# Key turns of the second head group ahead of the scaling of the value results on VectorE

## The chip, the cores and the metric

The kernel runs on one core of one Trainium2 chip. The metric is the device time of a run in microseconds (us), from the first to the last instruction with what the launch adds; the time of a kernel is the median of several runs.

## The reference

Two layers are applied twice to a small state `x` of 4 sequences with one token each (D = 512): attention against a cache of keys and values, then a gated feed-forward. The second round uses the same weights and the same caches.

```python
def _A_ref(x, k_cache, v_cache, wq, wo):          # 32 query heads, 8 key/value heads
    q = (x @ wq).reshape(B, Sq, Hq, Dh) ...        # Dh = 128
    scores = jnp.einsum("bhqd,bhkd->bhqk", q, k) * (Dh ** -0.5)   # 4096 cached keys
    p = _softmax(scores, axis=-1)
    o = jnp.einsum("bhqk,bhkd->bhqd", p, v)
    return o.reshape(B, Sq, Hq * Dh) @ wo
def _B_ref(x, w_gate, w_up, w_down):               # F = 1792
    return (_gelu(x @ w_gate) * (x @ w_up)) @ w_down

x = x + _A_ref(_layernorm(x), ...)
x = x + _B_ref(_layernorm(x), ...)
x = x + _A_ref(_layernorm(x), ...)
x = x + _B_ref(_layernorm(x), ...)
```

## The kernel before

All data is bfloat16. The caches of one sequence hold 8 heads of 4096 x 128 elements each for keys and for values, 8 MB apiece, and are the bulk of what is moved: 114 MB in all. The kernel works sequence by sequence and interleaves the second attention of one sequence with the first attention of the next, so that the keys and values stream without a long stop. `attend(b2, b1, ...)` (line 523) does this for the pair: `b2` is the sequence in its second attention (none in the first call), `b1` the next one in its first. It is called four times, for `b1` = 0 to 3; these calls are "attention 0" to "attention 3" here. The eight key/value heads go in two groups of four; `ga` and `gb` are the first and second group of `b1`. `attend_last` and `dense` do the last second attention and the feed-forward.

Keys and values are cut into tiles of 512 KB: half of one head of one sequence, `t` = 0 or 1. A key tile comes from DMA with the keys along the partitions, and VectorE turns it in place, as 32-bit words in blocks of 32 x 32: `Keys.turn` (line 373, the instruction on line 378, one for each tile, in the order in which tiles were loaded). For the second group this order is head by head, both halves of a head together, so the eight turns are (head 0, t 0), (head 0, t 1), (head 1, t 0) and so on. `scores(sc, g, t)` (line 383) then multiplies the four heads' halves t by the queries: 16 matmuls on line 389. The four of each round go over the four heads, so the first half, t = 0, needs the turns number 1, 3, 5 and 7, and the second half needs number 8 as well.

`soft` (line 393) takes the maximum on VectorE and the exponential on ScalarE, `soft_turn` and `soft_swap` bring the probabilities into the layout of the values, and `Values.step(n)` (line 492) makes n value units: one unit is one value tile times its probabilities, 16 matmuls on line 506 into the accumulator `ot`, of which there are two. After every fourth unit (after every second near the end of a sequence) VectorE scales the accumulated result by the reciprocal of the softmax sum and writes it to `OT_bf`: line 514. `out_proj` (line 276) reads `OT_bf` later.

Value tiles are loaded into a ring of seven tiles (`load_v`, line 467). A load is issued on the single DMA queue as soon as a slot is free, and a slot is freed when the unit that read it is done (`release`, line 464). Key tiles have places of their own and are loaded again when the scores that read them are done.

The order of instructions on each engine is the order in which the code names them; nothing rearranges it (`tc.manual_schedule()`, line 81). [...]

The place of the change is the middle of `attend`, lines 599 to 604. Ahead of it, turns 1 and 2 of the second group have been made, the softmax of the first group is done, and the queries for the second group are built. Line 599 makes turn 3, line 600 makes five value units on TensorE with one scaling on VectorE behind the fourth, line 601 makes turns 4 to 7, line 603 the first half of the scores, line 604 turn 8.

Of the kernel before, what the change touches and what calls it, by code (L numbers as in the profile page):

```python
# [30 lines left out]
def kernel(  # L31
# [224 lines left out]
    def build_q1(b, g):  # L256
        q_build(q_spread(q1_bf[:, g, :, b], amask, g), g)
# [95 lines left out]
    class Keys:  # L353
# [19 lines left out]
        def turn(self, count=1):  # L373
            for _ in range(count):
                kvh, t = self.tile(self.nt)
                self.nt += 1
                words = KT[kvh][t].rearrange("p c d -> p (c d)").bitcast(FP32)
                nc.vector.transpose(out=words, in_=words)  # L378

    def new_scores(bank):  # L380
        return ps_sc.tile([P, CH, QS], FP32, name="sc", tag=f"sc{bank}")
# [141 lines left out]
    def attend(b2, b1, next_q=None, rest=None):  # L523
# [4 lines left out]
        turn = keys.turn  # L528
# [67 lines left out]
        if first:  # L596
            q_first(q_rows(0, B, 1), 1, rstd1)
        build_q1(b1, gb)
        turn()
        vals.step(5)  # L600
        turn(4)
        sc1 = new_scores(0)
        scores(sc1, gb, 0)
        turn()
# [99 lines left out]
    x_bf = tmpp.tile([P, D], BF16, name="x_bf", tag="pp")  # L704
    dq.dma_start(out=x_bf[:B, :], in_=A_x.flatten_outer_dims())
    proj, prev = attend(None, 0)
    for b in range(B):
        fill = (lambda n: None) if prev is None else prev.step
        dense(b, 1, proj, fill)
        ln_square(b, 1)  # L710
        fill(1)
        mv = ln_center(b, 1)
        fill(1)
        ga, gb = groups(b + 1)
        qr0 = q_rows(b, 1, ga)
        rstd = ln_rstd(1, mv)
        am = small.tile([P, QD], FP32, name="am", tag="am")
        nc.vector.tensor_scalar(out=am[:], in0=amask[:], scalar1=rstd[:, 0:1], scalar2=None,
                                op0=ALU.mult)
        qm0 = q_spread(turn_rows(qr0, 512)[:, :, 0], am, ga)  # L720
        fill(2)
        q_build(qm0, ga)
        fill(1)

        def next_q():
            return q_spread(turn_rows(q_rows(b, 1, gb), 512)[:, :, 0], am, gb)

        if b < B - 1:
            proj, prev = attend(b, b + 1, next_q, fill)
        else:  # L730
            proj = attend_last(b, next_q, fill)
# [41 lines left out]
```

## Time and profile before

Three runs took 338.26, 335.23 and 338.08 us; the median is 338.08 us. The profiled execution has a span of 337.1 us, to which all profile times refer.

| what | us | number | mean ns |
|---|---|---|---|
| key turns, VectorE, L378 | 75.4 | 64 | 1218 |
| value units, TensorE, L506 | 62.8 | 1920 matmuls | 166 |
| scores, TensorE, L389 | 62.0 | 512 matmuls | 535 |
| scalings of value results, VectorE, L514 | 6.5 | 40 | 163 |
| VectorE idle ahead of L514 | 41.9 | | |
| VectorE idle ahead of L378 | 3.4 | | |
| TensorE idle ahead of L389 | 25.1 | | |
| DMA, share of 16 engines | 86.9% | 113.53 MB | |

"Busy" sums the durations of instructions; matmuls overlap in the array, so 16 of them take less than 16 times their mean. "Idle ahead of" an instruction is the time in which its engine did nothing just before it, put down to what ended it. In the timelines, a row merges instructions of one line that follow each other; its columns are start, duration, engine, line, operation, tiles, count, and in brackets the idle time ahead with its releaser. In the chain of waits the columns are start, duration and what ran. The memory traffic comes to 337 GB/s over the span, and to some 410 to 420 GB/s where nothing stops it.

### The profile page before, as it was taken

The page shows a single profiled execution, that of the slowest core. Times are in us where ns is not written, and L with a number is a line of the kernel's source. Part 1 is how long each engine was busy: PE and PEld are TensorE (multiplying, and loading weights), DVE is VectorE, ACT ScalarE, POOL GpSimd, SP SyncE. Part 2 cuts the span into 40 slices and gives each one's busy share as a digit, 9 for nine tenths or more (in the row PEclk, how much of TensorE's full clock was granted, in tenths as well). Part 3 has the DMA queues.
Part 4 walks back from the last instruction along what each step waited for, and adds up shares of the span by engine and source line. Part 5 has one row for each costly group of instructions (what it writes and reads, how often), then busy time and mean ns, then how long its engine had stood idle before and what let it go on. Part 6 is the DMA issues. An engine that isn't in the chain of part 4 may idle for free.

```text
span 337.1 us, 8603 instructions
## 1 busy us (share of the span) xinstructions
PE 209.5 (62%) x3844; PEld 121.4 (36%) x3844; DVE 171.1 (51%) x481; ACT 29.1 (9%) x70; POOL 0.7 (0%) x6
## 2 busy tenths in 40 slices
PE   1343275243587144989874539799763378798875
PEld 0011234121334122466441324564511236464655
DVE  5666262013439276425477774354787453544233
ACT  0003001000010010210010103000101012001100
POOL 0000000000000000000000000000000000000000
PEclk9996555555576555555585555555955575559555
DMA  7999976999759999589989994899999967999920
GB/s 273 423 416 419 412 302 239 351 379 379 304 136 420 419 421 386 218 321 380 366 296 414 421 382 170 318 403 399 370 424 418 416 213 269 410 373 379 413 82 2
DMA packets 27317, 114.07 MB, mean 338 GB/s; under 512 B 2312, under 2 KB 8208, under 8 KB 19984
## 3 DMA queue, kind: packets, MB, share of 16 engines
q1 hardware_dynamic: 27280, 113.53, 86.9%
q8 instruction: 30, 0.49, 0.6%
q14 instruction: 7, 0.06, 0.0%
HBM read 113.51 MB, written 0.00 MB: 337 GB/s over the span
## 4 chain that ended last, share of the span: by engine, by line
DMA 46%; PE 25%; DVE 16%; SPq 8%; issue 2%; ACT 2%; DVEq 0%
DMA ring<-in_A_v_cache_dram 30%; DMA kt<-in_A_k_cache_dram 13%; PE sc L389 8%; PE ot L506 6%; DVE kt L378 5%; DMA wd_sb<-in_B_w_down_dram 3%; SPq L134 3%; SPq L128 3%; PE rows L315 2%; PE y L348 2%; PE rows L226 2%; DVE pp L416 2%; ACT pp L408 1%; PE x L435 1%; DVE rows L216 1%
## 5 line engine op out<-in xcount | busy, mean ns | idle before, releaser
L506 PE MATMUL ot<-pe,ring 128*128 128x4 bf16 x1920 | 62.8, 166 | 35.5 <-DMA ring<-in_A_v_cache_dram 34.6
L506 PEld LDWEIGHTS <-ring 128*128 128x128 bf16 x1920 | 59.9, 105 | 65.1 <-DMA ring<-in_A_v_cache_dram 42.1
L389 PE MATMUL sc<-kt,qb 128*32 128x512 bf16 x512 | 62.0, 535 | 25.1 <-DVE kt L378 22.0
L378 DVE STREAM_TRANSPOSE kt<-kt 128x1024 f32<-128x1024 f32 x64 | 75.4, 1218 | 3.4 <-DMA kt<-in_A_k_cache_dram 3.4
L389 PEld LDWEIGHTS <-qb 128*32 128x32 bf16 x512 | 17.2, 114 | 53.6 <-issue 30.4
L216 DVE STREAM_TRANSPOSE rows<-rows 128x512 f32<-128x512 f32 (+1 forms) x23 | 16.2, 706 | 39.0 <-PE rows L226 19.1
L514 DVE TENSOR_TENSOR OT_bf<-ot,rden 128x8 bf16<-128x8 f32 (+1 forms) x40 | 6.5, 163 | 41.9 <-PE ot L506 41.4
L408 ACT ACTIVATE pp<-sc,nm 128x512 bf16<-128x512 f32 x16 | 11.0, 687 | 181.7 <-DVE junk L404 112.2
L395 DVE TENSOR_REDUCE m<-sc 128x1 f32<-128x512 f32 x16 | 10.8, 678 | 26.5 <-PE sc L389 26.5
L435 PE MATMUL x<-pp,ident_bf 128*32 128x128 bf16 x256 | 9.0, 282 | 22.1 <-DVE pp L416 21.8
L281 PE MATMUL rows<-wo_sb,OT_bf 128*1 128x512 bf16 (+1 forms) x136 | 16.5, 582 | 8.5 <-DMA wo_sb<-in_A_wo_dram 7.3
L226 PE MATMUL rows<-wq_sb,xn_bf 128*1 128x512 bf16 (+1 forms) x160 | 18.0, 595 | 4.6 <-DMA wq_sb<-in_A_wq_dram 4.3
L435 PEld LDWEIGHTS <-ident_bf 128*32 128x32 bf16 x256 | 6.5, 118 | 27.9 <-issue 25.9
L416 DVE STREAM_TRANSPOSE pp<-pp 128x512 bf16<-128x512 bf16 x16 | 11.2, 703 | 7.3 <-ACT pp L408 7.3
L438 ACT CAST pe<-x 128x512 bf16<-128x512 f32 x16 | 9.4, 586 | 18.6 <-PE x L435 18.6
L348 PE MATMUL y<-H_bf,wd_sb 128*128 128x1 bf16 (+1 forms) x280 | 8.6, 166 | 2.8 <-DVE H_bf L341 1.5
L348 PEld LDWEIGHTS <-wd_sb 128*128 128x128 bf16 x280 | 8.1, 104 | 4.1 <-DMA wd_sb<-in_B_w_down_dram 3.1
L247 PE MATMUL qe<-qm,t_bf 128*128 128x64 bf16 x16 | 3.4, 213 | 9.3 <-DVE qm L237 7.1
L250 DVE TENSOR_TENSOR qb<-qe,amask 128x256 bf16<-128x256 f32 x16 | 6.8, 425 | 4.7 <-PE qe L247 4.7
L226 PEld LDWEIGHTS <-xn_bf 128*1 128x1 bf16 (+1 forms) x160 | 4.5, 110 | 12.9 <-issue 11.7
L421 PE MATMUL den<-zx,mean_f 128*128 128x16 f32 x32 | 8.9, 357 | 0.0
L315 PE MATMUL rows<-wu_sb,xn_bf 128*1 128x448 bf16 x64 | 6.7, 567 | 2.9 <-DMA wu_sb<-in_B_w_up_dram 2.9
(78 smaller groups left out, 121.9 us busy)
## 6 DMA issues: line engine op xcount, KB each, us to landing
ring<-in_A_v_cache_dram SPq DMA_DIRECT2D x37, 1024.0 KB, 8.9
ring<-in_A_v_cache_dram SPq DMA_DIRECT2D x44, 512.0 KB, 7.0
kt<-in_A_k_cache_dram SPq DMA_DIRECT2D x20, 1024.0 KB, 14.3
kt<-in_A_k_cache_dram SPq DMA_DIRECT2D x24, 512.0 KB, 8.4
wq_sb<-in_A_wq_dram SPq DMA_DIRECT2D x2, 2048.0 KB, 20.2
wo_sb<-in_A_wo_dram SPq DMA_DIRECT2D x4, 1024.0 KB, 12.2
kt<-in_A_v_cache_dram SPq DMA_DIRECT2D x8, 512.0 KB, 9.8
wg_sb<-in_B_w_gate_dram SPq DMA_DIRECT2D x1, 1792.0 KB
```

What stands on the lines that cost most here:

```text
L216: nc.vector.transpose(out=rows[:, :n], in_=rows[:, :n])
L226: nc.tensor.matmul(rows[j * QS:j * QS + nb, :], lhsT=xn_bf[:, k, bs], rhs=w, start=(k == 0), stop=(k == KD - 1))
L281: nc.tensor.matmul(rows[r0:r0 + lhsT.shape[-1], :], lhsT=lhsT, rhs=wo_sb[:, i, :], start=(start and n < QD), stop=(stop and n >= hp - QD))
L315: nc.tensor.matmul(rows[j * QS:j * QS + nb, :KF * QS], lhsT=xn_bf[:, k, bs], rhs=w[:, j], start=(k == 0), stop=(k == KD - 1))
L348: nc.tensor.matmul(y[:, k], lhsT=wd_sb[:, c, k * P:(k + 1) * P], rhs=H_bf[:, c, :], start=(c == 0 and k == 0), stop=(c == KF - 1), skip_gr ...
L378: nc.vector.transpose(out=words, in_=words)
L389: nc.tensor.matmul(sc[s * QS:(s + 1) * QS], lhsT=qb[:, w0:w0 + 2 * W], rhs=kt[:, :, be // 2, :, be % 2], start=(t == 0 and be == 0), stop= ...
L395: nc.vector.tensor_reduce(out=m[:], in_=sc.rearrange("p c j -> p (c j)"), axis=AX.X, op=ALU.max)
L408: nc.scalar.activation(out=pp[:], in_=sc[:], func=ACT.Exp, bias=nm[:, 0:1], scale=scale, accum_out=ls[:])
L416: nc.vector.transpose(out=flat, in_=flat)
L435: nc.tensor.matmul(x[a * QS:(a + 1) * QS, s], lhsT=ident_bf[:, s * QS:(s + 1) * QS], rhs=pT[:, a], start=True, stop=True, skip_group_check ...
L506: nc.tensor.matmul(self.ot[:, s % 2], lhsT=v[:, i, :], rhs=pe[:, s, c, :], start=(c == 0), stop=(c == C - 1), skip_group_check=True)
```

## The change

The four turns that stood behind the five value units are made ahead of them, together with the one that was there already. TensorE's order stays as it was: five value units, then the first half of the scores. On VectorE the first scaling of value results of each attention comes after turn 7 instead of after turn 3. The aim is that VectorE does not wait for TensorE's value units while it has loaded key tiles to turn.

```diff
         build_q1(b1, gb)
-        turn()
+        turn(5)
         vals.step(5)
-        turn(4)
         sc1 = new_scores(0)
         scores(sc1, gb, 0)
         turn()
```

## The prediction

> **What bounds the kernel now.** I read the page first (engine shares and slices), then the chain of waits, then the timelines of TensorE and VectorE around the four places that the edit touches, and last the DMA rate in those windows. The page says that no engine is full and that the DMA engines come nearest:
>
> ```profile
> PE 209.5 (62%) x3844; PEld 121.4 (36%) x3844; DVE 171.1 (51%) x481; ACT 29.1 (9%) x70; POOL 0.7 (0%) x6
> ...
> q1 hardware_dynamic: 27280, 113.53, 86.9%
> ...
> DMA 46%; PE 25%; DVE 16%; SPq 8%; issue 2%; ACT 2%; DVEq 0%
> ```
>
> DMA is busy for 86.9% of 337.1 us, some 293 us, so about 44 us are left in which it stands still, and the chain that ended last leaves DMA for more than half of its length. The kernel alternates: DMA streams until the value ring is full, then a stretch of TensorE and VectorE work decides when ring slots come free again. A saving counts only in such a stretch. The chain, in order of time, shows one in attention of sequence 1:
>
> ```profile
> 111.16 17.43 DMA ring<-in_A_v_cache_dram
> 128.63 1.03 PE ot L506 x32
> 129.85 4.54 DVE kt L378 x4
> 134.43 1.87 PE sc L389 x13
> 136.30 0.52 PE ot L506 x16
> 136.82 1.85 PE sc L389 x16
> ...
> 143.05 1.44 PE ot L506 x48
> 144.50 7.82 DMA ring<-in_A_v_cache_dram
> ```
>
> Value tiles arrive, TensorE makes the fourth value unit, VectorE then scales (L514) and only then makes four key turns of 1.14 us, and the scores wait for them. The same "DVE kt L378 x4, 4.54" stands in the chain at 41.22, 129.85, 196.55 and 265.82 us: once in each of the four attentions, and nowhere else with that length. The VectorE timeline tells why the turns are late:
>
> ```profile
> 125.30 1.24 DVE L378 STREAM_TRANSPOSE kt<-kt 128x1024 f32<-128x1024 f32 x1
> 129.68 0.17 DVE L514 TENSOR_TENSOR OT_bf<-ot,rden 128x8 bf16<-128x8 f32 x1 [3.15 <-PE ot L506]
> 129.77 5.74 DVE L378 STREAM_TRANSPOSE kt<-kt 128x1024 f32<-128x1024 f32 x5
> ```
>
> VectorE idles 3.15 us for TensorE with the turns standing behind the scaling; the five turns then run without a gap, so their keys had landed. On TensorE it reads:
>
> ```profile
> 131.09 0.59 PE L506 MATMUL ot<-pe,ring 128*128 128x4 bf16 x16 [1.45 <-DMA ring<-in_A_v_cache_dram]
> 131.62 1.15 PE L389 MATMUL sc<-kt,qb 128*32 128x512 bf16 x3
> 134.43 1.87 PE L389 MATMUL sc<-kt,qb 128*32 128x512 bf16 x13 [1.67 <-DVE kt L378]
> 136.23 0.59 PE L506 MATMUL ot<-pe,ring 128*128 128x4 bf16 x16
> 136.75 1.90 PE L389 MATMUL sc<-kt,qb 128*32 128x512 bf16 x16
> ```
>
> [...] loaded keys were not turned in the 3.15 us of waiting. [...] The trace shows 0.50 at all four places until 272 us, so I price matmuls as found there[...].
>
> **The change part by part.** Nothing is added or taken away: VectorE has the same instructions, and in each of four attentions the first scaling of value results moves behind four key turns. TensorE's and the DMA queue's order stay.
>
> (1) The turns. They can start when the turn before the scaling ends. VectorE's idle time before L514 is 6.19, 3.15, 2.06 and 4.97 us at the four places, so that moment is 41.05-6.19 = 34.86, 129.68-3.15 = 126.53, 194.32 and 260.68 us. Four turns take 4.6 us (5.74/5 x 4, with their gaps), so they end at 39.5, 131.1, 198.9 and 265.3 instead of 45.8, 134.4, 201.1 and 270.4. Keys: in attentions 1 to 3 they are queued ahead of value tiles that TensorE had used by those moments; in attention 0 they come just ahead of a value pair used at 37.51, which may hold the turns some us, inside 6.19 us of slack.
>
> (2) The scaling. It now starts at the later of its matmuls and the turns: at 131.1 instead of 129.7 in attention 1, at 198.9 instead of 196.4 in attention 2, unchanged in the others. Who waits for it: its result goes to the output projection, first at 139.52 us in attention 1, some 8 us later, and it frees one of two accumulators, wanted again at the ninth unit, at 143.05. The one turn queued behind it (the eighth tile) ends about 132.4, and the second score half, which needs it, starts after 134. So the delay costs nothing.
>
> (3) The scores. TensorE's fifth value unit still waits for its value tile from DMA, so the first score half still starts at 43.04, 131.62, 198.76 and 267.61. Its 16 matmuls end at 47.67, 136.30, 203.00 and 272.27 by the chain, that is 4.63, 4.68, 4.24 and 4.66 us later. With all keys turned the same 16 take 1.90 us: the second half, at 136.75, shows it. In attention 2 the fourth of them needs a turn that ends 0.1 us after the first starts, which the three ahead of it cover. The saving is 2.73 + 2.78 + 2.34 + 2.76 = 10.6 us, and this is the disputed size: the wait that the trace names is only 1.67 us. I take the difference of the ends, since three early matmuls drawn out over 1.15 us are not 1.15 us of array work when 13 take 1.87.
>
> (4) What follows. Unit 6, the second half, two units, the softmax of L395 to L438 and then the ninth unit all hang in one chain, from 136.3 to 144.5 in attention 1, where the ring's next load is released. Does DMA let this move forward? Two windows of attention 1 tell (start and end, length, busy us and instructions of the five engines, TensorE's clock, DMA share, GB/s):
>
> ```profile
> 126.00:136.00 10.00, 5.27 (x96) 3.05 (x96) 6.36 (x7) 0.00 (x0) 0.00 (x0) 0.50 1.01 396
> 136.00:146.00 10.00, 9.40 (x181) 5.79 (x181) 4.41 (x15) 3.34 (x8) 0.00 (x0) 0.50 0.48 159
> ```
>
> DMA is full up to about 136 and then idle for half of ten us: (1-0.48) x 10 = 5.2 us. The same view of attentions 0, 2 and 3 (48 to 57, 203 to 212 and 272 to 281 us, shares 0.43, 0.41 and 0.46) gives 5.1, 5.3 and 4.9 us. Each is above the 2.3 to 2.8 us to be taken out, so the idle time shrinks to about 2.4 us and the loads after it start earlier by the whole saving. The values used in between are there: the stream up to 136 brings a pair in about 2.46 us (128.63, then 131.09), so units 7 and 8 land near 133.6 and are wanted near 135.9. After each stretch the chain runs on through loads which it released itself, so the four savings add.
>
> Sum: 338.08 - 10.6 = 327.5 us.
>
> **The rivals.** (B) The saving is only the wait that is named. For it: it is the trace's own figure, 1.67 at each place; if the three early matmuls really need their 1.15 us, the rest follows with its 1.87. Against it: the undisturbed 16 in 1.90. Time: 338.08 - 4 x 1.67 = 331.4 us. (C) DMA takes it back: the value stream, full ahead of the stretch, is the true limit, and TensorE only waits for values 2.7 us sooner. For it: 86.9% DMA, 42.1 us of weight loads waiting for the ring. Against it: about 5 us of idle DMA just behind each place. Time: 338.1 us. (D) Keys are late, and the scaling and all behind it wait for them. For it: turns wait for keys 5 times, 3.4 us in total, longest 1.5. Against it: none of these stands at the four places, where turns run on without a gap. If all 3.4 us were added: 341.5 us, slower. (E) [...] In attention 3, where it is granted from 274 on, the way from the first half's end to the next load takes 280.24-272.27 = 7.97 us against 8.20 in attention 1; three more of these give 0.7 us, 326.8 us.
>
> **How the numbers follow.** My forecast with (E), which is inside its width, 0.83; (B) 0.11; (C) 0.03; (D) 0.03. The time is 327.5 us. The range takes in (B) at the top, 331.4, and at the bottom the spread of the three times before: the fastest, 335.23, less 10.6 is 324.6. Low 324.6, high 331.5. Faster by over 1% follows from the forecast, (E) and (B), 0.94; within 1% from (C), 0.03; slower from (D), 0.03.
>
> **What would show it.** In the profile after: VectorE's timeline has four turns, then the scaling, with its idle time nearly gone in attentions 1 and 2; the first score half is 16 matmuls in 1.9 us behind the fifth unit with no wait for L378; the chain has no "DVE kt L378 x4" of 4.54 us there; the idle DMA behind each place is near 2.4 us. Wrong would be a value wait on unit 6 or 7 instead (C), a first half of 3 us (B), or turns waiting for keys (D).

## The result, and the profile after

The changed kernel took 326.22 us (median of four runs, 323.41 to 328.01) against 336.98 us for the kernel before (four runs, 335.23 to 338.26). The ratio is 0.9676, with a 95% interval from 0.9587 to 0.9765: 10.8 us faster. The prediction was 327.5 us. Of all runs reported below, one of the kernel before, at 341.5 us, is over 1.5% above the fastest of its kernel and is left out as slow.

The page of the kernel after, in its three lines on engines, DMA and the chain of waits:

```profile
PE 207.2 (64%) x3844; PEld 120.9 (37%) x3844; DVE 170.2 (53%) x481; ACT 29.1 (9%) x70; POOL 0.7 (0%) x6
...
q1 hardware_dynamic: 27280, 113.53, 89.8%
...
DMA 52%; PE 25%; DVE 9%; SPq 8%; ACT 2%; issue 2%; DVEq 0%
```

The instruction counts are the same, and so, nearly, are the busy times. What changed is VectorE's share of the chain, 9% where it was 16%. Its part shrank by some 25 us (0.16 x 337.1 - 0.09 x 324.0): the span became 13.1 us shorter, and most of the rest is now time in which the chain waits for DMA. The chain of waits in order of time, attention 1:

```profile
114.84 13.04 DMA ring<-in_A_v_cache_dram
127.93 0.59 PE ot L506 x16
128.51 1.83 PE sc L389 x16
130.34 0.52 PE ot L506 x16
130.86 1.67 PE sc L389 x15
...
136.92 1.44 PE ot L506 x48
138.37 7.82 DMA ring<-in_A_v_cache_dram
```

The four key turns of 4.54 us are gone from it. What releases the first score half is now the fifth value unit, and what released that is its value tile. VectorE's timeline shows where the turns went:

```profile
122.13 5.74 DVE L378 STREAM_TRANSPOSE kt<-kt 128x1024 f32<-128x1024 f32 x5
127.79 0.12 DVE L514 TENSOR_TENSOR OT_bf<-ot,rden 128x8 bf16<-128x8 f32 x1
```

Five turns run in one go, and the scaling follows with no idle time; its matmuls had ended at 126.45 us. And on TensorE:

```profile
127.93 0.59 PE L506 MATMUL ot<-pe,ring 128*128 128x4 bf16 x16 [1.47 <-DMA ring<-in_A_v_cache_dram]
128.44 1.90 PE L389 MATMUL sc<-kt,qb 128*32 128x512 bf16 x16
130.27 0.59 PE L506 MATMUL ot<-pe,ring 128*128 128x4 bf16 x16
```

All 16 matmuls of the first half stand in one row of 1.90 us. From the fifth unit to the sixth it is 130.27-127.93 = 2.34 us; before it was 136.23-131.09 = 5.14 us. I call this the place interval: it holds nothing but the fifth unit and the first score half. DMA, by two windows that part near the end of the first score half (130.3 us here), as those shown of before did (136.3 us); the last columns are TensorE's clock, DMA share and GB/s:

```profile
120.00:130.00 10.00, 5.42 (x115) 3.64 (x114) 8.64 (x11) 0.59 (x1) 0.00 (x0) 0.50 1.01 418
130.00:140.00 10.00, 8.66 (x189) 5.69 (x186) 4.45 (x15) 3.34 (x8) 0.00 (x0) 0.67 0.76 284
```

DMA is as full as before ahead of the place (1.01 both times). Behind it, the idle time is (1-0.76) x 10 = 2.4 us where it was 5.2. In attentions 0, 2 and 3, in nine us from 45.4, 192.9 and 258.8 us on, the shares are 0.77, 0.78 and 0.80, so 1.8 to 2.1 us are idle where it was 4.9 to 5.3. The time that the turns gave back came out of DMA's idle time.

### The profile page after: what moved, and what is told of

It is laid out like the page before. It is cut to its first block, busy times and chain, and to the rows that moved or that the text cites. A ratio compares the mean times of both kernels' runs of the same rounds, so it can differ in the third digit from the quotient of the medians.

```text
span 324.0 us, 8603 instructions
## 1 busy us (share of the span) xinstructions
PE 207.2 (64%) x3844; PEld 120.9 (37%) x3844; DVE 170.2 (53%) x481; ACT 29.1 (9%) x70; POOL 0.7 (0%) x6
## 4 chain that ended last, share of the span: by engine, by line
DMA 52%; PE 25%; DVE 9%; SPq 8%; ACT 2%; issue 2%; DVEq 0%
DMA ring<-in_A_v_cache_dram 36%; DMA kt<-in_A_k_cache_dram 13%; PE sc L389 8%; PE ot L506 7%; DMA wd_sb<-in_B_w_down_dram 3%; SPq L134 3%; SPq L128 3%; PE y L348 2%; PE rows L315 2%; DVE pp L416 2%; PE rows L226 2%; PE x L435 2%; ACT pp L408 1%; PE rows L281 1%; ACT pe L438 1%
## 5 line engine op out<-in xcount | busy, mean ns | idle before, releaser
L389 PE MATMUL sc<-kt,qb 128*32 128x512 bf16 x512 | 59.1, 544 | 15.6 <-DVE kt L378 12.5
L395 DVE TENSOR_REDUCE m<-sc 128x1 f32<-128x512 f32 x16 | 10.8, 678 | 30.2 <-PE sc L389 30.2
L226 PE MATMUL rows<-wq_sb,xn_bf 128*1 128x512 bf16 (+1 forms) x160 | 18.9, 622 | 4.9 <-DMA wq_sb<-in_A_wq_dram 4.6
L226 PEld LDWEIGHTS <-xn_bf 128*1 128x1 bf16 (+1 forms) x160 | 4.5, 110 | 13.1 <-issue 11.7
```

Of the source, the lines that this page charges most:

```text
L226: nc.tensor.matmul(rows[j * QS:j * QS + nb, :], lhsT=xn_bf[:, k, bs], rhs=w, start=(k == 0), stop=(k == KD - 1))
L389: nc.tensor.matmul(sc[s * QS:(s + 1) * QS], lhsT=qb[:, w0:w0 + 2 * W], rhs=kt[:, :, be // 2, :, be % 2], start=(t == 0 and be == 0), stop= ...
```

## The experiments

The theory was that the first score half has to wait for the turns that stand behind the scaling, each worth its 1.15 us until the values set the end, and that DMA hands all of it on. Its rivals were that only the named wait of 1.67 us counts, and that the gain came from DMA or the clock. The first four kernels were run together; their common measure is the kernel before at 336.43 us (seven runs), and their edits are shown against it.

**One more turn behind the scaling.**

```diff
-        turn()
         vals.step(5)
-        turn(4)
+        turn(5)
```

> The opposite of the change: all five turns (3 to 7) stand behind the scaling of value results, one more than before. Theory (the turns behind the waiting scaling set the end of the first score half, each worth its 1.15 us at each of four places, and DMA hands all of it on): 4 x 1.15 = 4.6 us slower than before, about 341.6 us against 337.0; from the fifth value unit's start to the end of the first score half 1.15 us longer at each place. Rival (the gain measured came from the DMA stream or the clock, not from the turns): no change within 1 us.

It took 340.93 us, ratio 1.0116 (1.0076 to 1.0156): 4.5 us slower, as the theory has it. TensorE's timeline in attention 1:

```profile
131.76 0.59 PE L506 MATMUL ot<-pe,ring 128*128 128x4 bf16 x16 [1.47 <-DMA ring<-in_A_v_cache_dram]
132.28 0.61 PE L389 MATMUL sc<-kt,qb 128*32 128x512 bf16 x2
133.96 0.58 PE L389 MATMUL sc<-kt,qb 128*32 128x512 bf16 x1 [1.07 <-DVE kt L378]
136.21 1.86 PE L389 MATMUL sc<-kt,qb 128*32 128x512 bf16 x13 [1.67 <-DVE kt L378]
138.00 0.59 PE L506 MATMUL ot<-pe,ring 128*128 128x4 bf16 x16
```

The last named wait is 1.67 us, as before, though the place is 1.1 us longer: another turn's wait has come in ahead of it. A single wait in brackets was never the size of the loss.

**One turn fewer behind the scaling.**

```diff
-        turn()
+        turn(2)
         vals.step(5)
-        turn(4)
+        turn(3)
```

> A quarter of the change: one turn (number 4) moved ahead of the scaling, three left behind it. Theory: the last turn ends 1.15 us sooner at each place, 4.6 us faster than before, about 332.4 us. Rival (only the wait that the trace names counts, 1.67 us at each place): the same 4.6 us, since 1.15 is below 1.67, so this run does not tell these two apart; rival (DMA or clock): no change within 1 us.

It took 332.2 us, ratio 0.9859 (0.982 to 0.9898): 4.2 us faster. The rival of DMA or clock, which expected no change within 1 us here and in the run before, is out.

**Two turns fewer behind it.**

```diff
-        turn()
+        turn(3)
         vals.step(5)
-        turn(4)
+        turn(2)
```

> Half of the change: turns 4 and 5 moved ahead of the scaling, 6 and 7 left behind it. Theory (each place saves the smaller of 2 x 1.15 = 2.3 us and its 2.73, 2.78, 2.34, 2.76 us): 4 x 2.3 = 9.2 us faster than before, about 327.8 us, nearly all that the whole change brought. Rival (only the named wait of 1.67 us counts): 4 x 1.67 = 6.7 us faster, 330.3 us. Rival (proportional to the turns moved): half of the whole change's 10.8, 5.4 us, 331.6 us.

It took 327.7 us, ratio 0.9747 (0.9702 to 0.9792): 8.7 us faster, with an interval from 7.0 to 10.0 us. The rivals' 6.7 us (the named wait) and 5.4 us (in proportion) lie outside it, the theory's 9.2 inside. Half of the turns moved brings most of the gain, because the rest is hidden behind the fifth value unit. In attention 1 the first half takes 2.41 us instead of 1.90, in one row and with no named wait at all:

```profile
129.14 0.59 PE L506 MATMUL ot<-pe,ring 128*128 128x4 bf16 x16 [1.47 <-DMA ring<-in_A_v_cache_dram]
129.66 2.41 PE L389 MATMUL sc<-kt,qb 128*32 128x512 bf16 x16
```

**The old order without the wait.** The scaling stays in front of the turns, but does not read the value sums (the eight heads of that scaling come out as other numbers; all else is made as before).

```diff
-                        in0=self.ot[:, s0 % 2:s0 % 2 + m], in1=rden[:, s0:s0 + m], op=ALU.mult)
+                        in0=(rden[:, s0:s0 + m] if not last and self.n == 2 * NT
+                             else self.ot[:, s0 % 2:s0 % 2 + m]), in1=rden[:, s0:s0 + m], op=ALU.mult)
```

> The order of before, but the first scaling of each attention's value results takes the softmax reciprocals in place of the value sums, so it waits for no value unit; the eight heads of that scaling therefore come out as other numbers, everything else is made as before. Theory (it is the scaling's wait for TensorE that holds the turns, not the place of the turns as such): as fast as the change, 10.6 us faster than before, about 326.4 us, with VectorE's four turns ahead of the fifth value unit. Rival (the turns themselves, in their place, are late for another reason, such as keys not landed or the accumulator's release): no more than 1 us faster.

It took 327.1 us, ratio 0.9695 (0.9644 to 0.9747): 9.3 us faster, and the 10.6 us of the theory lie within the interval (8.5 to 12.0). VectorE's timeline, attention 1:

```profile
122.06 1.23 DVE L378 STREAM_TRANSPOSE kt<-kt 128x1024 f32<-128x1024 f32 x1
123.22 0.12 DVE L514 TENSOR_TENSOR OT_bf<-rden 128x8 bf16<-128x8 f32 x1
123.26 5.74 DVE L378 STREAM_TRANSPOSE kt<-kt 128x1024 f32<-128x1024 f32 x5
```

The scaling runs for 0.12 us between the turns and nothing is lost. So it was neither the scaling's own time nor its place, but its wait for TensorE with loaded keys queued behind it.

The place intervals of all these kernels, from the fifth to the sixth value unit's start in TensorE's timeline of each profile, in us:

| kernel | att. 0 | att. 1 | att. 2 | att. 3 | sum | sum against before | time against before |
|---|---|---|---|---|---|---|---|
| five turns behind | 6.22 | 6.24 | 5.81 | 6.24 | 24.51 | +4.50 | +4.5 |
| four behind (before) | 5.08 | 5.14 | 4.68 | 5.11 | 20.01 | | |
| three behind | 3.95 | 3.98 | 3.56 | 3.97 | 15.46 | -4.55 | -4.2 |
| two behind | 2.83 | 2.87 | 2.50 | 2.85 | 11.05 | -8.96 | -8.7 |
| none behind (the change) | 2.34 | 2.34 | 2.44 | 2.34 | 9.46 | -10.55 | -10.8 |
| four behind, no wait | 2.35 | 2.35 | 2.50 | 2.35 | 9.55 | -10.46 | -9.3 |

The times in the last column are differences of medians; the measured ratios put the same gains up to 1 us apart from them (10.3 instead of 9.3 us for the last row). Within this width the times follow the sums through a range of 15 us. This shows both the size and that DMA hands it on.

**What binds next.** With the change, the scores wait for the values of the units ahead of them (1.47 us ahead of the fifth unit in attention 1). So I let the scores overtake units. The change was timed again as the measure, and the edits are shown against the change, except where another kernel is named.

> The change itself, timed once more beside the two kernels below, so that these are read against it on the same chip. Theory: 10.6 us faster than before, about 326.0 us. The savings at the four places, from the fifth value unit's start to the end of the first score half, are 2.7, 2.8, 2.3 and 2.8 us; what a profile shows beyond their sum is the DMA stream's and the clock's scatter and does not repeat.

It took 327.01 us against 337.24 us for the kernel before (ratio 0.9726, 0.9663 to 0.9788), and its intervals are 2.35, 2.35, 2.43 and 2.35 us.

```diff
-        vals.step(5)
+        vals.step(4)
         sc1 = new_scores(0)
         scores(sc1, gb, 0)
         turn()
-        vals.step(1)
         scores(sc1, gb, 1)
...
-        vals.step(2)
+        vals.step(4)
         soft_turn(p0)
```

> The change, and on TensorE both score halves of the second head group stand behind the fourth value unit; units 5 to 8 come behind the scores, in the shadow of the softmax. Theory (the next limit at these places is TensorE's order: the scores wait for the fifth and sixth unit's values from DMA, while the keys are turned): the second half ends about 2.4 us sooner than with the change in attentions 0 and 3, 1.1 in attention 1 and 0.5 in attention 2, where the turns end only 0.1 to 1.4 us ahead of that; 6.4 us faster than the change if DMA, idle for about 2.1 us behind each place with the change, hands it all on: about 320 us. Rival (the value stream is now the limit, for units 5 to 8 free their ring places later): no faster than the change, 326 us or above.

It took 325.85 us, 1.2 us less than the change and not clear of its scatter. The expected 6.4 us did not come; the result is nearer to the rival, that the value stream is now the limit. I measured the whole stretch, from the start of the fourth unit's row (where that holds units 3 and 4, from there) to the first matmul of the feed-forward (of the output projection in attention 0), against the change timed beside it: 20.50 against 21.51 us, 22.49 against 22.23, 23.98 against 21.73 and 19.98 against 22.12. So attentions 0 and 3, where the turns end early, gain 1.0 and 2.1 us, and attention 2 loses 2.3. TensorE's timeline of this kernel in attention 2:

```profile
187.46 0.59 PE L506 MATMUL ot<-pe,ring 128*128 128x4 bf16 x16 [1.58 <-DMA ring<-in_A_v_cache_dram]
187.98 1.15 PE L389 MATMUL sc<-kt,qb 128*32 128x512 bf16 x3
190.79 3.57 PE L389 MATMUL sc<-kt,qb 128*32 128x512 bf16 x29 [1.67 <-DVE kt L378]
194.29 1.86 PE L506 MATMUL ot<-pe,ring 128*128 128x4 bf16 x64
```

The scores wait for turns, and units 5 to 8 wait behind the scores with their ring places taken. Two windows of this attention, first for the change as it was timed again, then for this kernel:

```profile
188.00:198.00 10.00, 6.38 (x116) 3.67 (x120) 6.85 (x9) 0.00 (x0) 0.00 (x0) 0.50 1.01 408
198.00:208.00 10.00, 9.04 (x177) 5.52 (x176) 4.56 (x17) 3.34 (x8) 0.00 (x0) 0.50 0.74 276
```

```profile
188.00:198.00 10.00, 8.33 (x126) 3.99 (x128) 6.68 (x13) 1.09 (x3) 0.00 (x0) 0.50 0.72 275
198.00:208.00 10.00, 7.07 (x159) 4.90 (x152) 3.06 (x11) 2.16 (x5) 0.00 (x0) 0.50 0.98 394
```

DMA's idle time did not shrink ((1-0.72 + 1-0.98) x 10 = 3.0 us against 2.6); it moved to where the ring places are held. I read this as the gain going back through the ring; a ring with more places, which would test it by itself, was not run.

The scores still earlier, behind the second unit (edit against the kernel just shown):

```diff
-        vals.step(4)
+        vals.step(2)
         sc1 = new_scores(0)
...
-        vals.step(4)
+        vals.step(6)
         soft_turn(p0)
```

> As the one before, but the scores stand already behind the second value unit, so units 3 to 8 come behind them. Theory: in attention 0 the turns end near 39.5 us, ahead of the third unit's values, and the scores gain another 1.5 us; in attentions 1 and 2 the scores wait for the turns, which end no sooner, while loaded values lie in the ring and their six places come free 3 to 5 us later, more than the 2.1 us for which DMA is idle there, so the stream stops: slower than the one before by 2 to 6 us, 322 to 326 us. Rival (TensorE's order alone counts, the ring does not bind): at least as fast as the one before, 320 us or less.

It took 331.13 us (16 runs), 5.3 us more than with the scores behind the fourth unit: within the 2 to 6 us expected, though above the 322 to 326 us, since the kernel it builds on had missed its own time by as much. The chain of waits in attention 2 shows the ring at work. Units 3 to 8 run only behind the scores; the next load into the ring is released when the third of them ends (48 matmuls), and the eleventh unit runs when that load has landed:

```profile
194.08 3.57 PE sc L389 x29
197.65 1.34 PE ot L506 x48
...
199.00 7.37 DMA ring<-in_A_v_cache_dram
...
206.42 0.60 PE ot L506 x16
```

In TensorE's timelines the eleventh unit waits 2.41, 2.32 and 3.63 us for its tile in attentions 1, 2 and 3; with the change it does not wait.

Then only the first half ahead of the fifth unit, with the change timed once more beside it.

```diff
-        vals.step(5)
+        vals.step(4)
         sc1 = new_scores(0)
         scores(sc1, gb, 0)
         turn()
-        vals.step(1)
+        vals.step(2)
         scores(sc1, gb, 1)
```

> The change once more, as the measure for the kernel below on the same chip: 10.6 us faster than before, 326 to 327 us.

> The change, and on TensorE only the first score half moves ahead of the fifth value unit; units 5 and 6 come between the halves, so that their ring places come free at most 1 us later than with the change. Theory (scores that wait for values cost the same way as scores that wait for turns, as long as ring places do not come free later): the second half ends 1.4 us sooner in attentions 0 and 3, at the same time in attention 1 and 0.5 later in attention 2, where the turns end too late; 2.3 us faster than the change, about 324.5 us. Rival (the stream of values now sets the time of these stretches, so nothing on TensorE is handed on): the change's time within 1 us.

The change took 326.21 us (ratio to before 0.9695, 0.9648 to 0.9742), this kernel 324.53 us (0.9628, 0.9583 to 0.9673). The difference of the means of six runs each is 2.2 us with a standard error of 0.76, that of the medians 1.7: small, but beyond the scatter, and near the 2.3 us expected. By the stretches, against the change beside it, attention 0 gained 1.6 us, attention 1 lost 0.1, attention 2 lost 1.3 and attention 3 gained 1.6: together 1.8 us, with more lost in attention 2 than the 0.5 expected.

Last, an order for each attention:

```diff
-        vals.step(5)
+        n1, n2 = {0: (4, 2), 3: (4, 0)}.get(b1, (5, 1))
+        vals.step(n1)
...
-        vals.step(1)
+        vals.step(n2)
...
-        vals.step(2)
+        vals.step(8 - n1 - n2)
```

> The change, with TensorE's order picked for each attention by what the two runs of it showed: in attention 0 the first score half behind the fourth value unit and units 5 and 6 between the halves (1.6 us shorter there, from the second value pair to the output projection), in attention 3 both halves behind the fourth unit (2.1 us shorter from there to the feed-forward), in attentions 1 and 2, where the turns end too late and the same orders cost 0.1 to 2.2 us, as in the change. Theory (the savings of single attentions add): 3.7 us faster than the change, about 322.8 us. Rival (they don't add, since what one attention saves the value stream takes back in the next): no faster than the kernel with one order for all, 324.5 us or more.

> The change once more, as the measure for the kernel above: 326 to 327 us.

It took 323.24 us, ratio to before 0.961 (0.9571 to 0.9649); the change beside it took 325.47 us (0.9679, 0.9647 to 0.9712). The difference of the means is 2.7 us (standard error 0.77), of the medians 2.2, below the 3.7 expected. Attention 0 gave 0.8 us instead of 1.6, attention 3 gave 1.4 instead of 2.1; both stretches hold waits for loads, and the length of such a stretch differs between profiles of one kernel: in attention 3 it is 22.12, 22.28 and 21.65 us in three timings of the change. By its median it is the fastest kernel measured here. It is ahead of the change beside it by more than the scatter; whether it beats the kernel with one order for all is not settled, since the two were not run side by side.

## Why the prediction was right

Time and range: 327.5 us was predicted in 324.6 to 331.5; 326.22 us was measured. The saving was predicted at 10.6 us and measured at 10.8, and at 10.2, 10.3 and 10.6 us in the three repetitions. Of the 1.3 us between the two times 1.1 are the starting point: the prediction took the kernel before at 338.08 us, the median of three runs; with a fourth it is 336.98 us.

(1) The turns: right. In all four attentions they run without a gap, five in 5.74 us, in attention 0 too, where the prediction held a delay by late keys possible. In attentions 1 and 2 the scaling begins as they end. In attentions 0 and 3 it still waits 1.65 and 0.35 us for TensorE, with only turn 8 behind it.

(2) The delayed scaling costs nothing: right. Against the fifth unit it runs later in attentions 1 and 2; the second score half, which needs the turn behind it, and the ninth unit, which needs the accumulator that it frees, start without a wait in all four attentions.

(3) The scores: right in mechanism and in size. I chose the difference of the ends, 2.73 + 2.78 + 2.34 + 2.76 us, over the named wait of 1.67 us; the place intervals shrank by 2.74, 2.80, 2.24 and 2.77 us. Attention 2 was 0.1 us short: there the turns end as the first half starts, and it takes 1.99 us instead of 1.90, which the prediction took as covered by the three matmuls ahead.

(4) What follows: right. DMA's idle time behind attention 1 fell to the predicted 2.4 us, and units 6 to 8 waited for no value tile.

Rival (B), 6.7 us, is excluded by the kernel with two turns behind the scaling and by the change itself (7.9 to 13.9 us by its interval), (C) by the agreement of times and intervals, (D) by the timelines: the turns run without a gap. (E) was my assumption that the full clock, recorded in attention 3 of before from 274 us on, would be granted in more stretches; no run shows what raises it. In the window behind the place of attention 1 the recorded clock is 0.67 where it was 0.50 before, but the way from the first half's end to the next load took 138.37-130.34 = 8.03 us there against 8.20, hardly shorter. Step (1) took the turns behind the scaling as held up while it waits, and the timelines show this: in attention 0, with five, four, three and two turns behind the scaling, VectorE is idle for 7.35, 6.19, 5.41 and 4.32 us ahead of it, and the first of these turns starts 0.08 to 0.09 us after the scaling does.

One thing does not fit at first sight: the two profiled spans differ by 337.1-324.0 = 13.1 us, more than the place intervals give. The profiled execution of before was one of the longest of its kernel, 339.0 us against a median of 336.98. From the first scores of the call, at 165.57 us, to the fifth unit of attention 2 it needs 32.7 us; the profiles of the change, its repetitions and the four kernels with other places of the turns or no wait need 30.9 to 32.1. That stretch is the stream of keys and values; why it was longer in that execution stays open.

## What to carry to other kernels

Behind an instruction that waits for another engine, look at what its own engine could already do: here 0.17 us of work held up 4.6 us of ready work, four times. The size of the loss was the interval from the last thing that stays to the end of the work that was held up, compared with the same work undisturbed (10.55 us over the four places, against 10.8 us of time); the wait named at its last instruction was 0.6 to 0.7 of it, and stayed the same when the loss grew. Once such a wait is gone, ask what the next reordering holds back: moving both score halves ahead of four value units kept ring places taken and brought 1.2 us where 6.4 were expected, while one half ahead of two units brought about what was expected.

## What had not been expected

The savings of this order are so regular that each turn moved, as long as it is not hidden, is worth between 1.06 and 1.16 us at every place, while repeated runs of one kernel scatter by 1 to 5 us. Where that scatter comes from is not shown.

A run's mean granted clock does not help to find out, for its record is not what it seems. In the profile of the change TensorE's clock is given as 1.00 from the start to 50.2 us; yet in attention 0, at 43.22 us, the 16 matmuls of the first score half take 1.90 us, as they do in attention 1 at a recorded 0.50. At 164.84 us of the same profile, again at a recorded 1.00, 32 score matmuls take 2.00 us. So here the first value of the record does not tell how fast TensorE worked. In the profile of before it ends at 28.2 us. Of the difference between the mean clocks of these two profiles, 0.587 and 0.625, about 0.03 comes from this alone (an estimate, with 0.50 as the clock that is hidden: (50.2-28.2) x 0.5 / 324.0). The place interval of attention 0 is 2.34 or 2.35 us in all four timings of the change, as in attention 1; in the profile above the record has 1.00 at the one place and 0.50 at the other.
